# Fused S5 and MLP kernel: the skip D*xn written into PSUM ahead of Y's matmuls, w1's first loads split, a new order by hand

## The chip, the cores and the metric

The kernel runs on one core of a Trainium2 chip. The metric is the device time of one execution in microseconds (us). A core has five engines, each with its own instruction stream: TensorE (PE: matmuls, with weight loads shown as PEld), VectorE (DVE), ScalarE (ACT), GpSimd (POOL) and SyncE (SP, which here only issues transfers). They work side by side and wait for one another through semaphores. Matmuls write to PSUM, which has eight banks of 512 float32 per partition; everything else lies in SBUF. Transfers are done by 16 DMA engines; an instruction on SP or ScalarE only starts one.

## The reference, cut to what matters

```python
def _A_ref(x, Lambda_re, Lambda_im, B_re, B_im, C_re, C_im, log_dt, Dskip):
    Lam = Lambda_re + 1j * Lambda_im
    Lam_bar = jnp.exp(jnp.exp(log_dt) * Lam)
    B_bar = ((Lam_bar - 1.0) / Lam)[:, None] * (B_re + 1j * B_im)
    Bu = jnp.einsum("bld,pd->blp", x + 0j, B_bar)
    for t in range(L):
        h = Lam_bar[None, :] * h + Bu[:, t, :]
        hs.append(h)
    y = 2.0 * jnp.einsum("blp,dp->bld", jnp.stack(hs, 1), C_re + 1j * C_im).real + x * Dskip
    return y

def _B_ref(x, w1, b1, w2, b2):
    h = _gelu(jnp.einsum("bsd,df->bsf", _layernorm(x), w1) + b1)
    return jnp.einsum("bsf,fd->bsd", h, w2) + b2

xn = _layernorm(A_x)
s = _A_ref(xn, ...)
g = _silu(_B_ref(xn, ...))
return A_x + s * g
```

There are L = 2048 tokens, D = 448 channels and F = 1792 hidden units, in bfloat16. D*xn is the last term of y, called the skip here.

## The kernel before, in words

The tokens run in four groups of 512 (g = 0 to 3), each of two blocks of 256. Within a block, even and odd time steps are kept apart ("par"): the recurrence is scanned over pairs of steps, and y is made for even and odd steps by different matrices. All activations are kept transposed, channels on the partitions. 448 channels are three full tiles of 128 (j = 0, 1, 2) and one of 64 (j = 3); the last holds even and odd steps in its two halves of partitions.

What one group goes through:

- norms: `xn` (for the S5 branch) and `xn2` (for the MLP) by VectorE and ScalarE, then a transposing transfer each on SP's queue to `xnT` and `xn2T` (step words L and N).
- the first MLP stage (words m, L661): matmuls of w1 into pairs of PSUM banks, gelu by ScalarE to `gT` (L667). w1 has 448 rows: three tiles of 128, and 64 rows that are loaded by a transfer of their own (key `w1r`); VectorE or ScalarE copies the other 64 rows next to them (keys `w1c_0` to `w1c_3`). Group 0 runs this stage first by blocks, in 256 columns, behind a front of parameter work.
- the second MLP stage (words W, L783 for j < 3, L786 for j = 3): gT times w2, silu by ScalarE to the gate `g_sb` (L789).
- Bu (words b, L690): transposed B (`BT`, three transfers, made from `Bn` and the products `LB`) times xnT. Job 0 reads the first two BT transfers, job 1 the last. ScalarE or VectorE copies the sums to `ue` and `u_sb`.
- the scan (words S): VectorE turns, scans (L749) and turns back; the results are `hx` (odd) and `hz` (even).
- y (words Y, function `yt`): for j < 3 seven matmuls with `CZ` and hx for the odd columns of a bank (L805), seven with `CQ` and hz for the even ones (L806); for j = 3 seven and seven into the two halves of partitions (L813, L814). Then D*xn is added and the sum times the gate is written to `t3`, called t in the profile (L828). In Y0 to Y2, and in one of Y3's four, VectorE adds D*xn while it copies the bank to `tmp` (L826). In the other three of Y3 PE adds it, by a matmul with a diagonal matrix `Dg` of D (L808, L816), which `skips()` builds.
- out: for groups 0 to 2 (words O) two transposing transfers of t back, then VectorE adds x (L842, L845), then output transfers. Group 3 (words P, `out_pe`) is transposed by PE (L855), and VectorE adds x from PSUM (L861); the outputs leave in two pairs, one transfer of each on SP's queue and one on ScalarE's.

Nothing is scheduled while it runs. Every step is a task with keys that it reads and writes; the table `ORDER` gives the order in which the tasks are issued to their engines, and `SECOND` names the tasks that run on the second of their two possible engines. A word of `STEPS` says which task is made: `Y03d2` is y of group 0, tile 3, by VectorE ("d"; "p" is by PE), in bank 2. Each engine works through its own tasks in order, so a task that waits holds back all behind it on its engine, and a transfer on SP's queue those behind it on that queue.

D and b2 come as two rows and are turned into columns `dcol` and `b2c` (together `db`) by small matmuls on PE (`skip_columns`, L554, L555), which stand in the middle of group 0's first MLP stage. The rows are loaded behind all of w1 on SP's queue.

Of the kernel before, what the change touches and what calls it, by code (L numbers as in the profile page):

```python
# [7 lines left out]
ACT = mybir.ActivationFunctionType  # L8
# [189 lines left out]
def bass_recurrent_scan__ssm_conv_s5__mixer_channel_mlp__prompt_kernel(  # L198
# [18 lines left out]
    with ExitStack() as es:  # L217
# [21 lines left out]
        Dg = SB("Dg", [128, 4, 128])  # L239
# [5 lines left out]
        yD = tmp  # L245
# [58 lines left out]
        with nc.Block():  # L304
# [49 lines left out]
            for i, vec in enumerate((A_Dskip, B_b2)):  # L354
                ld("sp", drows[i:i + 1, :], dram_ap(vec, 0, [[D, 1], [1, D]]), [f"dbr{i}"])
# [23 lines left out]
            def first_stats(b):  # L379
                for par in range(2):  # L380
# [5 lines left out]
                    if b == 0:  # L386
                        kb.add("act", [lambda e, var=var, r1=r1: e.activation(r1, var, ACT.Ln, scale=1.0 + LN_EPS, bias=eps[:, 1:2]),
                                       lambda e, r1=r1: e.activation(r1, r1, ACT.Exp, scale=-0.5)], [f"mv0_{q}", "eps", "warm"], [f"r1{q}"], chain=True)
                    elif par == 1:
                        vs2, rs2 = lnmv[:, 0, 1:4:2, 1], lnw[:, 0, 2, 1, 1:4:2]  # L390
                        kb.add("act", [lambda e: e.activation(rs2, vs2, ACT.Ln, scale=1.0 + LN_EPS, bias=eps[:, 1:2]),
                                       lambda e: e.activation(rs2, rs2, ACT.Exp, scale=-0.5)], ["mv0_1", "mv0_3", "eps", "warm"], ["r11", "r13"], chain=True)
# [166 lines left out]
            def skips():  # L559
                for j in range(4):  # L560
                    small(lambda e, j=j: e.tensor_scalar(Dg[:, j, :], ident[:], dcol[:, j:j + 1], None, op0=ALU.mult), ["ident", "db"], [f"Dg{j}"])

            def tables():
# [9 lines left out]
                for k, (dst, src, sc, bias) in enumerate((  # L573
# [6 lines left out]
                        RA + ["rb", "Ws0", "sgn1", "sgn2", "sgn3"], ["W"] + (RA + ["rb"] if k == 4 else []))  # L580
# [3 lines left out]

            tslot = [0]
# [63 lines left out]
            def mm1_phase(g, b, j, pair, second):  # L649
# [9 lines left out]
                def one_mm(k, n, h):  # L659
# [3 lines left out]
                   xk2 + [f"w1_{c}", "w1r"] + ([f"w1c_{c}"] if second else []), [f"ps{bk[0]}", f"ps{bk[1]}"], split=True)  # L663
# [71 lines left out]
            def ssm(g):  # L735
                hb = g % 2
                W, SF = ["W"], ["sf0", "sf1"]
# [53 lines left out]
            ybank = [0]  # L791

            def yt(g, j, by_pe, bk):

                gx = hb = g % 2
                ybank[0] += 1
# [4 lines left out]
                xt_k = [f"xnT{gx}"]  # L801
                ko = [f"hx{hb}", f"hy{hb}"] + [f"CZ{k}" for k in range(7)]
                ke = [f"hz{hb}"] + [f"CQ{k}" for k in range(7)]
                if j < 3:
                    pe([lambda e, k=k: e.matmul(par(psum[:, bk, :], 1), CZ[:, k, cols], halves(hx[:, hb, k, 1:NK + 1]), start=k == 0, stop=k == 6) for k in range(7)], ko, [f"ps{bk}"])  # L805
                    fns = [lambda e, k=k: e.matmul(par(psum[:, bk, :], 0), CQ[:, k, cols], halves(hz[:, hb, k, :]), start=not by_pe and k == 0, stop=not by_pe and k == 6, skip_group_check=by_pe) for k in range(7)]  # L806
                    if by_pe:
                        fns.append(lambda e: e.matmul(P.rearrange("p (q c) -> p q c", q=4), Dg[:, j, :], xr, start=False, stop=True, skip_group_check=True))  # L808
# [162 lines left out]
```

## Time and profile before

| | us |
|---|---|
| median of three runs | 147.08 (147.01 to 148.35) |
| the profiled execution: its span | 145.3 |
| PE busy in it | 138.8 |
| VectorE busy | 130.1 |
| ScalarE busy | 100.5 |
| GpSimd busy | 26.0 |

The profile is of one execution. Its span runs from the first instruction to the last; a run's time also holds what lies around the span. Rows name an instruction by line, engine, operation, and output and input tiles; the name of a tile leaves out its number, so all PSUM banks are "psum", and some buffers carry the name of the memory they share: w_sb is w1 or w2, `xn_sb` both norms, `dk` also holds the rows of D and b2, `Bn` also holds hz and the outputs, and `Cr` also holds the transposed t. "<-" in brackets or behind a bar gives what ended the wait ahead of an instruction. A chain of waits is followed back from the last instruction to what released it.

### The profile page before, as it was taken

The numbers are of one execution on the slowest core, as the hardware profiler recorded it, in microseconds if no ns is written. First come the engines' busy times: TensorE is split into PE (matmuls) and PEld (weight loads), VectorE is DVE, ScalarE is ACT, GpSimd is POOL, SyncE is SP. The second block draws the span as 40 slices with busy tenths as digits, with TensorE's granted clock in tenths as the row PEclk, the third lists the DMA queues.
The fourth block names the chain that finished last, engine by engine and source line by source line (L and its number), as shares of the span: only waits on it lengthen the run. The fifth ranks groups of instructions, "written<-read, shape, count | busy, mean of one in ns | idle before, by whom it ended". The sixth has DMA issues, their size and how long they took to land.

```text
span 145.3 us, 3626 instructions
## 1 busy us (share of the span) xinstructions
PE 138.8 (95%) x1457; PEld 91.9 (63%) x1461; DVE 130.1 (90%) x284; ACT 100.5 (69%) x184; POOL 26.0 (18%) x76
## 2 busy tenths in 40 slices
PE   7879999999999999999999999999999999999990
PEld 7757764464444477776768644877766668744870
DVE  2898999899999799899999999798699999999782
ACT  3588889998889466799999690594559993086200
POOL 4354315154500017000020000300000710000000
PEclk9999999999999999999999999999999999999999
DMA  4959990899999990000000074819800100201434
GB/s 104 299 173 242 351 366 19 162 226 95 210 210 215 122 241 11 5 2 5 0 0 5 18 144 89 163 23 187 192 7 0 68 0 0 82 4 23 95 116 126
DMA packets 38610, 15.98 MB, mean 110 GB/s; under 512 B 33145, under 2 KB 38146, under 8 KB 38594
## 3 DMA queue, kind: packets, MB, share of 16 engines
q1 hardware_dynamic: 38036, 15.52, 48.7%
q10 hardware_dynamic: 558, 0.24, 0.6%
q8 instruction: 11, 0.18, 0.5%
q14 instruction: 5, 0.04, 0.1%
HBM read 5.86 MB, written 1.84 MB: 53 GB/s over the span
## 4 chain that ended last, share of the span: by engine, by line
PE 85%; DVE 4%; DMA 3%; SPq 3%; issue 2%; DVEq 0%
PE psum L661 29%; PE psum L783 25%; PE psum L690 15%; PE psum L805 6%; PE psum L786 4%; PE psum L806 4%; DMA dk<-in_B_b_dram 3%; SPq L78 3%; PE psum L813 2%; DVE t L828 2%; DVE tmp L826 1%; DVE Bn L861 1%; DVE Bn L842 0%; PE psum L855 0%; PE psum L814 0%
## 5 line engine op out<-in xcount | busy, mean ns | idle before, releaser
L661 PE MATMUL psum<-xn2T,w_sb 64*128 64x512 bf16 (+1 forms) x476 | 46.7, 340 | 1.0 <-DVE w_sb L302 0.8
L667 ACT ACTIVATE gT<-psum,b1f 128x512 bf16<-128x512 f32 (+1 forms) x68 | 37.4, 615 | 5.2 <-PE psum L661 5.1
L783 PE MATMUL psum<-gT,w_sb 128*128 128x512 bf16 x164 | 36.2, 379 | 0.4 <-issue 0.3
L661 PEld LDWEIGHTS psum<-xn2T,w_sb 64*128 64x128 bf16 x476 | 25.3, 108 | 15.6 <-PE psum L661 1.4
L783 PEld LDWEIGHTS psum<-gT,w_sb 128*128 128x128 bf16 x168 | 16.2, 98 | 19.8 <-ACT gT L667 1.1
L690 PE MATMUL psum<-xnT,BT 64*128 64x256 bf16 x392 | 24.5, 270 | 0.2 <-DVE tmp L826 0.2
L690 PEld LDWEIGHTS psum<-xnT,BT 64*128 64x128 bf16 x392 | 18.9, 94 | 6.1 <-DVE tmp L826 0.4
L749 DVE TENSOR_TENSOR_SCAN s_w<-vs,dk 128x786 f32<-128x786 bf16 (+1 forms) x8 | 16.3, 2058 | 0.1
L443 ACT ACTIVATE xn_sb<-x_all,lnw 128x448 bf16<-128x448 bf16 (+2 forms) x18 | 11.2, 670 | 5.3 <-DMA xnT<-xn_sb 5.2
L301 ACT ACTIVATE vs<-s_w 64x258 bf16<-64x258 f32 (+2 forms) x12 | 8.0, 686 | 8.0 <-DVE s_w L749 7.9
L789 ACT ACTIVATE g_sb<-psum,db 128x512 bf16<-128x512 f32 (+1 forms) x16 | 9.3, 623 | 4.5 <-PE psum L783 4.4
L826 DVE SCALAR_TENSOR_TENSOR tmp<-xnT,db,psum 128x512 f32<-128x512 bf16 (+1 forms) x16 | 10.1, 645 | 0.9 <-PE psum L814 0.7
L805 PE MATMUL psum<-hx,CZ 128*128 128x256 bf16 x84 | 10.8, 276 | 0.0
L758 POOL TENSOR_TENSOR ang<-s_w,ang 128x16 f32<-128x16 f32 x3 | 1.8, 616 | 49.2 <-ACT s_w L756 49.2
L806 PE MATMUL psum<-Bn,CQ 128*128 128x256 bf16 x84 | 10.5, 273 | 0.0
L465 ACT ACT_TABLE_LOAD x8 | 10.3, 1283 | 0.3
L805 PEld LDWEIGHTS psum<-hx,CZ 128*128 128x128 bf16 x84 | 8.0, 98 | 2.5 <-issue 0.6
L301 ACT ACTIVATE ue<-psum 128x512 bf16<-128x512 f32 (+1 forms) x13 | 6.8, 549 | 3.6 <-PE psum L690 3.6
L806 PEld LDWEIGHTS psum<-Bn,CQ 128*128 128x128 bf16 x84 | 8.1, 98 | 1.4 <-issue 0.4
L301 ACT ACTIVATE u_sb<-psum 128x512 bf16<-128x512 f32 (+1 forms) x14 | 6.0, 490 | 3.5 <-PE psum L690 3.4
L828 DVE TENSOR_TENSOR t<-tmp,g_sb 128x512 bf16<-128x512 f32 (+1 forms) x13 | 7.9, 622 | 0.0
L442 DVE TENSOR_SCALAR xn_sb<-x_all,lnw 128x448 bf16<-128x448 bf16 (+2 forms) x22 | 7.2, 361 | 0.5 <-DMA xnT<-xn_sb 0.3
(155 smaller groups left out, 183.7 us busy)
## 6 DMA issues: line engine op xcount, KB each, us to landing
x_all<-in_A_x_dram SPq DMA_DIRECT2D x3, 448.0 KB, 4.6
w_sb<-in_B_w_dram SPq DMA_DIRECT2D x3, 448.0 KB, 6.4
out_dram<-Bn SPq DMA_DIRECT2D x6, 224.0 KB, 2.4
w_sb<-in_B_w_dram SPq DMA_DIRECT2D x3, 384.0 KB, 5.1
w_sb<-in_B_w_dram SPq DMA_DIRECT2D x2, 224.0 KB, 5.0
Bn<-in_A_B_im_dram SPq DMA_DIRECT2D x1, 336.0 KB, 7.5
Bn<-in_A_B_re_dram SPq DMA_DIRECT2D x1, 336.0 KB, 8.0
x_all<-in_A_x_dram SPq DMA_DIRECT2D x2, 112.0 KB, 2.0
```

Of the source, the lines that this page charges most:

```text
L301: kb.either(("act", [lambda e, o=o, i=i: e.activation(o, i, ACT.Copy) for o, i in pairs]), ("dve", [lambda e, o=o, i=i: e.tensor_copy(o, i ...
L443: ("act", [lambda e, o=o, i=i: e.activation(o, i, ACT.Identity, bias=nb, scale=rs) for o, i in parts]),
L465: kb.add("act", lambda e: e.preload_act_table_set(what), reads, writes, sem=name)
L661: return lambda e: e.matmul(dst(bk[k]), w1_sb[rows, d, fcol(2 * j + k)], rhs[rows, d], start=not second and n == 0, stop=second and n == 3)
L667: act(lambda e, k=k, fi=fi: e.activation(gT[:, gb, fi, cols], psum[:, bk[k], cols], ACT.Gelu_apprx_tanh, bias=b1f[:, fi:fi + 1]), ["b1f", ...
L690: fns.append(lambda e, rows=rows, bank=bank, m=m, o=o, n=n: e.matmul(psum[:, bank, c * NK:(c + 1) * NK].rearrange("p (b c) -> p b c", b=2) ...
L749: dve(lambda e, so=so, vi=vi, di=di: e.tensor_tensor_scan(so, vi, di, 0.0, ALU.add, ALU.mult), ["v", "vl", "vz", "dk", "dk01"] + ["v3"] * ...
L783: pe([lambda e, fi=fi: e.matmul(psum[:, bk, :], w2_sb[:, fi, 128 * j:128 * j + 128], gT[:, gb, fi, :], start=fi == 0, stop=fi == NF - 1) f ...
L805: pe([lambda e, k=k: e.matmul(par(psum[:, bk, :], 1), CZ[:, k, cols], halves(hx[:, hb, k, 1:NK + 1]), start=k == 0, stop=k == 6) for k in ...
L806: fns = [lambda e, k=k: e.matmul(par(psum[:, bk, :], 0), CQ[:, k, cols], halves(hz[:, hb, k, :]), start=not by_pe and k == 0, stop=not by_ ...
L826: dve([lambda e, o=o, p=p, x=x, d=d: e.scalar_tensor_tensor(out=v(o), in0=x, scalar=d, in1=v(p), op0=ALU.mult, op1=ALU.add) for o, p, x, d ...
L828: dve(lambda e: e.tensor_tensor(t3[:, 512 * j:512 * j + n], s, g_sb[:, hb, 512 * j:512 * j + n], ALU.mult), [ks, f"g{hb}_{j}"], [f"t3{j}"])
```

## The change

The new `yt` writes D*xn into the whole bank first, by ScalarE (a copy with the column of D as scale) or by VectorE, whichever `SECOND` says; this is called the seed. All matmuls of y then add to it (none starts a bank anew), and t is read straight from PSUM. The evictions through `tmp`, the matmuls with `Dg`, `Dg` itself and `skips()` are gone. Of the 16 seeds, 14 run on ScalarE and two, the pairs of 64 x 256 of Y1 and Y2, on VectorE; ScalarE's are twelve of 128 x 512 and two pairs of 64 x 256.

The 64 rows of w1 come in two transfers, 768 and 1024 columns wide. SP's queue now starts, behind x, with the 256-column chunk of w1 and the first of these two. D and b2 are issued on ScalarE's queue. The key of the turning tables is split into five, `W0` to `W4`. A branch on `POWER`, which is False, does nothing. `ORDER` and `SECOND` are new throughout.

```diff
-            ld("sp", w1_sb[64:128, 3, :], dram_ap(B_w1, 384 * F, [[F, 64], [1, F]]), ["w1r"])
+            REST = ((0, 768), (768, 1024))
+            def ldrest(k):
+                a, w = REST[k]
+                ld("sp", w1_sb[64:128, 3, a:a + w], dram_ap(B_w1, 384 * F + a, [[F, 64], [1, w]]), [f"w1r{k}"])
             ldw1(0)
+            ldrest(0)
...
-            for c in range(1, 4):
-                ldw1(c)
+            for i, vec in enumerate((A_Dskip, B_b2)):
+                ld("act", drows[i:i + 1, :], dram_ap(vec, 0, [[D, 1], [1, D]]), [f"dbr{i}"])
+            ldw1(1)
+            ldw1(2)
+            ldrest(1)
+            ldw1(3)
...
-            for i, vec in enumerate((A_Dskip, B_b2)):
-                ld("sp", drows[i:i + 1, :], dram_ap(vec, 0, [[D, 1], [1, D]]), [f"dbr{i}"])
...
-            def skips():
-                for j in range(4):
-                    small(lambda e, j=j: e.tensor_scalar(Dg[:, j, :], ident[:], dcol[:, j:j + 1], None, op0=ALU.mult), ["ident", "db"], [f"Dg{j}"])
...
-            def yt(g, j, by_pe, bk):
+            def yt(g, j, bk):
...
+                seeds = [(P, xr, dcol[:, j:j + 1])]
+                if j == 3:
+                    seeds = [(P[h], xnT[h, gx, :, 4 * r + 3, :], dcol[h, 3:4]) for r, h in enumerate((slice(0, 64), slice(64, 128)))]
+                v = lambda t: t.rearrange("p (q c) -> p q c", c=128)
+                kb.either(("act", [lambda e, o=o, x=x, d=d: e.activation(v(o), x, ACT.Copy, scale=d) for o, x, d in seeds]),
+                          ("dve", [lambda e, o=o, x=x, d=d: e.tensor_scalar(v(o), x, d, None, op0=ALU.mult) for o, x, d in seeds]), ["db", f"xnT{gx}"], [f"ps{bk}"])
                 if j < 3:
-                    pe([... start=k == 0, stop=k == 6) for k in range(7)], ko, [f"ps{bk}"])
+                    pe([... start=False, stop=k == 6, skip_group_check=True) for k in range(7)], ko, [f"ps{bk}"])
...
-                    dve([lambda e, o=o, p=p, x=x, d=d: e.scalar_tensor_tensor(out=v(o), in0=x, scalar=d, in1=v(p), op0=ALU.mult, op1=ALU.add) for o, p, x, d in parts],
-                        [f"ps{bk}", "db"] + xt_k, [ks])
-                dve(lambda e: e.tensor_tensor(t3[:, 512 * j:512 * j + n], s, g_sb[:, hb, 512 * j:512 * j + n], ALU.mult), [ks, f"g{hb}_{j}"], [f"t3{j}"])
+                dve(lambda e: e.tensor_tensor(t3[:, 512 * j:512 * j + n], P, g_sb[:, hb, 512 * j:512 * j + n], ALU.mult), [f"ps{bk}", f"g{hb}_{j}"], [f"t3{j}"])
```

Line numbers of the changed kernel are some eight higher behind the loads: L669 is the first MLP stage (L661 before), L698 is Bu (L690), L791 and L794 are the second MLP stage (L783, L786), L812 is a seed by ScalarE, L815 and L816 are y's matmuls (L805, L806), and L675 is gelu.

The new order changes PE's rows most between the first MLP stage of group 1 and that of group 2. Before, PE had there (a row is an instruction, its output and inputs, its shape, and how many follow one another):

```order
L661 MATMUL psum<-xn2T,w_sb 128x512 x98
L783 MATMUL psum<-gT,w_sb 128x512 x42
L786 MATMUL psum<-gT,w_sb 64x256 x28
L690 MATMUL psum<-xnT,BT 128x256 x56
L661 MATMUL psum<-xn2T,w_sb 128x512 x12
L690 MATMUL psum<-xnT,BT 128x256 x42
```

Bu of group 0 came behind all of W1. Now the same place reads:

```order
L669 MATMUL psum<-xn2T,w_sb 128x512 x98
L698 MATMUL psum<-xnT,BT 128x256 x12
L791 MATMUL psum<-gT,w_sb 128x512 x14
L794 MATMUL psum<-gT,w_sb 64x256 x28
L698 MATMUL psum<-xnT,BT 128x256 x44
L791 MATMUL psum<-gT,w_sb 128x512 x28
L698 MATMUL psum<-xnT,BT 128x256 x42
L669 MATMUL psum<-xn2T,w_sb 128x512 x20
```

Twelve of Bu's matmuls moved right behind the first stage, and 44 into the midst of W1.

On SP's queue the transfers that Bu and y need (xnT of group 0; BT; C transposed, as Cr and CZ, from C's rows) stood before in this order:

```order
L77 DMA_TRANSPOSE xn2T<-xn_sb 128x16x128
L78 DMA Bn<-in_A_B_re_dram 64x448
L77 DMA_TRANSPOSE Cr<-in_A_C_re_dram 128x3x448
L78 DMA x_all<-in_A_x_dram 128x2x896
L77 DMA_TRANSPOSE Cr<-in_A_C_im_dram 128x1x448
L77 DMA_TRANSPOSE Cr<-in_A_C_im_dram 128x3x448
L77 DMA_TRANSPOSE CZ<-in_A_C_re_dram 128x1x448
L77 DMA_TRANSPOSE xnT<-xn_sb 128x16x128
L77 DMA_TRANSPOSE BT<-Bn 128x16x128 x2
L77 DMA_TRANSPOSE BT<-Bn 128x24x128
```

Now they stand so:

```order
L77 DMA_TRANSPOSE xn2T<-xn_sb 128x16x128
L78 DMA Bn<-in_A_B_re_dram 64x448
L78 DMA x_all<-in_A_x_dram 128x2x896
L77 DMA_TRANSPOSE xnT<-xn_sb 128x16x128
L77 DMA_TRANSPOSE Cr<-in_A_C_im_dram 128x3x448
L77 DMA_TRANSPOSE Cr<-in_A_C_re_dram 128x3x448
L77 DMA_TRANSPOSE BT<-Bn 128x16x128 x2
L77 DMA_TRANSPOSE Cr<-in_A_C_im_dram 128x1x448
L77 DMA_TRANSPOSE BT<-Bn 128x24x128
L77 DMA_TRANSPOSE CZ<-in_A_C_re_dram 128x1x448
```

xnT moved ahead of all parts of C, one part of C (128x1x448) behind the first two BT transfers, and another, CZ, behind the third.

On ScalarE the stretch from the end of group 2's first MLP stage to the silu table of that group held no work on y before:

```order
L443 ACTIVATE xn_sb<-x_all,lnw 128x128
L667 ACTIVATE gT<-psum,b1f 128x512 x4
L443 ACTIVATE xn_sb<-x_all,lnw 128x384
L443 ACTIVATE xn_sb<-x_all,lnw 128x128
L465 ACT_TABLE_LOAD
```

Now the seeds of Y0, and the first of Y1, stand between the last gelus there (u_sb are copies of Bu's sums):

```order
L675 ACTIVATE gT<-psum,b1f 128x512
L812 ACTIVATE psum<-xnT,db 128x512 x2
L300 ACTIVATE u_sb<-psum 128x2x256
L300 ACTIVATE u_sb<-psum 128x256
L675 ACTIVATE gT<-psum,b1f 128x512
L812 ACTIVATE psum<-xnT,db 128x512
L675 ACTIVATE gT<-psum,b1f 128x512
L812 ACTIVATE psum<-xnT,db 64x256 x2
L675 ACTIVATE gT<-psum,b1f 128x512
L812 ACTIVATE psum<-xnT,db 128x512
L476 ACT_TABLE_LOAD
```

Five seeds moved in among the gelus, ahead of the table load.

More of the change, by code (lines that the diff above doesn't have):

```diff
@@ L244, in bass_recurrent_scan__ssm_conv_s5__mixer_channel_mlp__prompt_kernel @@
         tmp = SB("tmp", [128, 2, 512], F32)
-        yD = tmp
         WT = SB("WT", [128, 4, 3, NW])
@@ L389, in first_stats @@
                     elif par == 1:
[L390 to L392 removed]
+                        vs2, rs2, ws2 = lnmv[:, 0, 1:4:2, 1], lnw[:, 0, 2, 1, 1:4:2], lnw[:, 0, 0, 1, 1:4:2]
+                        if POWER:
+                            kb.add("pool", [lambda e: e.tensor_scalar(ws2, vs2, 1.0 + LN_EPS, LN_EPS * LN_EPS, op0=ALU.mult, op1=ALU.add),
+                                            lambda e: e.tensor_tensor(rs2, ws2, mhalf[:, 0, :].to_broadcast([128, 2]), ALU.pow)], ["mv0_1", "mv0_3", "mhalf"], ["r11", "r13"], chain=True)
+                        else:
+                            kb.add("act", [lambda e: e.activation(rs2, vs2, ACT.Ln, scale=1.0 + LN_EPS, bias=eps[:, 1:2]),
+                                           lambda e: e.activation(rs2, rs2, ACT.Exp, scale=-0.5)], ["mv0_1", "mv0_3", "eps", "warm"], ["r11", "r13"], chain=True)
             def first_apply(b):
@@ L583, in tables @@
                 small([lambda e: e.memset(dk[:, :, 0:1], 0.0), lambda e: e.memset(dk[:, :, 1:LEAD], 1.0), lambda e: e.memset(dk[:, :, LEAD + NK:NS], 0.0)], [], ["dk01"] + old)
+            WK = [f"W{k}" for k in range(5)]
             tslot = [0]
@@ L800, in yt @@
                 xr = xnT[:, gx, :, j::4, :].rearrange("p b r c -> p (b r) c")
-                xt_k = [f"xnT{gx}"]
                 ko = [f"hx{hb}", f"hy{hb}"] + [f"CZ{k}" for k in range(7)]
                 ke = [f"hz{hb}"] + [f"CQ{k}" for k in range(7)]
-                if j < 3:
[L805 to L808, printed above, removed]
-                    pe(fns, ke + (xt_k + [f"Dg{j}"]) * by_pe, [f"ps{bk}"])
+                seeds = [(P, xr, dcol[:, j:j + 1])]
[4 more added lines that the diff above has]
+                          ("dve", [lambda e, o=o, x=x, d=d: e.tensor_scalar(v(o), x, d, None, op0=ALU.mult) for o, x, d in seeds]), ["db", f"xnT{gx}"], [f"ps{bk}"])
+                if j < 3:
+                    pe([lambda e, k=k: e.matmul(par(psum[:, bk, :], 1), CZ[:, k, cols], halves(hx[:, hb, k, 1:NK + 1]), start=False, stop=k == 6, skip_group_check=True) for k in range(7)], ko, [f"ps{bk}"])
+                    pe([lambda e, k=k: e.matmul(par(psum[:, bk, :], 0), CQ[:, k, cols], halves(hz[:, hb, k, :]), start=False, stop=k == 6, skip_group_check=True) for k in range(7)], ke, [f"ps{bk}"])
                 else:
@@ L812, in yt @@
                     for k in range(7):
[L813 to L828 removed]
+                        fns += [lambda e, k=k: e.matmul(psum[0:64, bk, 0:NK], CQ[:, k, cols], hz[:, hb, k, :], start=False, stop=k == 6, skip_group_check=True),
+                                lambda e, k=k: e.matmul(psum[64:128, bk, 0:NK], CZ[:, k, cols], hx[:, hb, k, 1:NK + 1], start=False, stop=k == 6, skip_group_check=True)]
+                    pe(fns, ko + ke, [f"ps{bk}"], split=True)
+                dve(lambda e: e.tensor_tensor(t3[:, 512 * j:512 * j + n], P, g_sb[:, hb, 512 * j:512 * j + n], ALU.mult), [f"ps{bk}", f"g{hb}_{j}"], [f"t3{j}"])
             OLD = [f"CQ{k}" for k in range(7)] + [f"CZ{k}" for k in range(7)]
@@ L880, in bass_recurrent_scan__ssm_conv_s5__mixer_channel_mlp__prompt_kernel @@
             first_stats(1)
-            gelu_table(0, ["cr", "r10", "r12", "r11", "r13"])
+            gelu_table(0, ["cr", "r10", "r12"] + ["r11", "r13"] * (not POWER))
             dummies(4, ["st0"])
```

36 lines of the change are left out of this document (10 added, 26 removed), and 36 rows, old and new, of the table ORDER.

## The prediction

> **What bounds the kernel now.** I read the page's busy line and its chain of what ended last, then the list of PE's waits, then a table by stage. Columns of the page's first line: busy us, share of the span, instructions.
>
> ```profile
> PE 138.8 (95%) x1457; PEld 91.9 (63%) x1461; DVE 130.1 (90%) x284; ACT 100.5 (69%) x184; POOL 26.0 (18%) x76
> PE 85%; DVE 4%; DMA 3%; SPq 3%; issue 2%; DVEq 0%
> ```
>
> PE is busy 95% of the span and is 85% of the chain. What it waited for (us in total, times, longest):
>
> ```profile
> PE psum L661 <- DVE w_sb L302: 0.8, 1, 0.8
> PE psum L554 <- DMA dk<-in_B_b_dram: 0.8, 1, 0.8
> PE psum L855 <- DVE t L828: 0.3, 1, 0.3
> PE psum L690 <- DVE tmp L826: 0.2, 1, 0.2
> ```
>
> The two waits of 0.8 us are both in the front, before 10.5 us; behind it PE has almost no holes. By stage (stretch, its length, then busy time of PE, PEld, DVE, ACT, POOL with instructions, clock, DMA share, GB/s):
>
> ```profile
> 5.40:10.50 5.10, 3.47 (x57) 2.64 (x55) 4.91 (x21) 4.03 (x10) 2.46 (x11) 1.00 0.78 209
> 20.70:31.40 10.70, 10.70 (x71) 5.46 (x72) 9.63 (x33) 10.50 (x16) 4.21 (x17) 1.00 0.63 134
> 31.40:42.50 11.10, 10.88 (x99) 5.22 (x97) 10.59 (x29) 9.38 (x16) 4.05 (x8) 1.00 1.12 184
> 42.50:53.30 10.80, 10.80 (x71) 5.35 (x72) 9.83 (x23) 7.77 (x12) 0.00 (x0) 1.00 1.19 193
> 53.30:74.70 21.40, 21.40 (x295) 15.03 (x296) 20.05 (x36) 18.52 (x34) 4.38 (x9) 1.00 0.08 16
> 91.00:97.60 6.60, 6.44 (x71) 5.02 (x68) 5.60 (x12) 5.06 (x9) 1.36 (x2) 1.00 0.50 97
> ```
>
> So work taken off VectorE is worth only what PE waits for it: 0.16 us in 91.00:97.60 (6.60 − 6.44). To move the end, an edit must start PE sooner, shorten PE's own work, or open a hole in it. The granted clock is 1.00 throughout. The profiled span is 145.3 us and the median of the three runs 147.08, so 1.8 us lie around the span; I keep those.
>
> **The front.** The timeline of all engines there, two rows of the chain (SP issues the 384 KB chunk at 2.19 and w1's last 64 rows at 2.67), and the sizes and landing times of three loads of w1:
>
> ```profile
> 2.19 0.43 SPq L78
> ...
> 2.67 0.59 SPq L78
> w_sb<-in_B_w_dram SPq DMA_DIRECT2D x1, 384.0 KB, 4.2
> w_sb<-in_B_w_dram SPq DMA_DIRECT2D x1, 224.0 KB, 4.8
> w_sb<-in_B_w_dram SPq DMA_DIRECT2D x1, 192.0 KB, 4.6
> 5.64 0.60 ACT L301 ACTIVATE xn2T<-psum 128x512 bf16<-128x512 bf16 x1 [0.41 <-PE psum L406]
> 6.80 0.42 DVE L302 COPY xn2T<-psum 128x512 bf16<-128x512 bf16 x1
> 7.25 0.29 DVE L302 COPY w_sb<-w_sb 64x512 bf16<-64x512 bf16 x1
> 7.50 1.90 PEld L661 LDWEIGHTS psum<-xn2T,w_sb 64*128 64x128 bf16 x34 [0.88 <-issue]
> 9.02 1.57 ACT L667 ACTIVATE gT<-psum,b1f 128x256 bf16<-128x256 f32 x4
> 10.48 0.21 PE L554 MATMUL psum<-ident,dk 2*128 2x2 bf16 x3 [0.81 <-DMA dk<-in_B_b_dram]
> ```
>
> PE's first weight load (7.50) comes before the DVE copy named as releaser ends (7.25 + 0.29 = 7.54), so that copy isn't it: the 64 rows are, 2.67 + 4.8 = 7.47. They were third behind the 384 KB chunk. Now 192 KB and 96 KB lead, 320 KB less. From the chunk's landing (issued at 2.19, so 6.4) to 7.47 224 KB took 1.07 us, 4.8 ns per KB; 320 KB less would give about 6.0. Next late is the second copy of xn2T, at 7.22 (6.80 + 0.42) on VectorE. It now runs on ScalarE straight behind the first, and ScalarE does the two rsqrt pairs before the parameter copy; I take 0.3 to 0.6 us off the transposes ahead, so the copies end near 6.6. PE starts near 6.7, 0.85 us sooner (bounds: 0.3, if only 7.22 is reached, and 1.5). The wait of 0.81 for b2 goes too, since D and b2 are issued on ScalarE's queue some 2 us sooner. But PE can't keep it: gelu began at 9.02, behind its table load, frees the three pairs of banks only from there on, and the copies of w1's 64 rows stand on VectorE behind the norm of the second tile. I expect the same 84 first matmuls to end 0.85 us sooner in all; bounds 0 (if those set the pace) and 1.7 (0.85 + 0.81). **Front: −0.85.**
>
> The Trainium skill's page "DMA: Bandwidth & Descriptors", section "Issuing engines are not separate DMA queues", speaks against the move of D and b2: loads from several engines share the same 16 DMA engines and only the issue time is saved. By it they might land near 10.3 as before (10.48 in the row above) and PE would stall again by some 0.2 us, which makes the sum 147.1; whether the small rows really overtake no run here shows.
>
> **Y and its seed.** Groups by form: busy us and mean ns behind the bar.
>
> ```profile
> L826 DVE SCALAR_TENSOR_TENSOR tmp<-xnT,db,psum 128x512 f32<-128x512 bf16 x10 | 7.2, 744 | 0.2
> L826 DVE SCALAR_TENSOR_TENSOR tmp<-xnT,db,psum 64x256 f32<-64x256 bf16 x6 | 2.9, 479 | 0.7 <-PE psum L814 0.7
> L594 ACT ACTIVATE tmp<-Bn,cw 128x512 f32<-128x512 bf16 x1 | 0.7, 709 | 0.0
> L301 ACT ACTIVATE ue<-psum 128x512 bf16<-128x512 f32 x10 | 6.0, 598 | 3.6 <-PE psum L690 3.6
> L301 ACT ACTIVATE u_sb<-psum 128x256 bf16<-128x256 f32 x7 | 2.4, 380 | 2.5 <-PE psum L690 2.4
> ```
>
> Removed from VectorE: 7.2 + 2.9 = 10.1 us of evictions; the four small builds of Dg, on VectorE and POOL and waited for by nobody in PE's list, go as well. Added: 16 seeds. Twelve of 128x512 and two pairs of 64x256 go to ScalarE, two pairs to VectorE (4 x 0.48 = 1.9 us). No such write into PSUM is in the trace. The nearest rows are L594 (same scale by a column, written to SBUF, 709) and L301 (598, without the scale); I take 0.65. ScalarE gets 12 x 0.65 + 4 x 0.38 = 9.3 us. VectorE's relief is worth the waits that name it: **−0.2**, bounds 0 and −0.5 (with L855's 0.3).
>
> A seed puts a link into the bank's cycle: before, Y's first matmul waited for the bank's last reader; now the seed waits for it, and the matmul for the seed. In Y2 and Y3 ScalarE has room. In 53.30:74.70 it is busy 18.52 of 21.40, so 2.9 us are free, and Y0's four seeds need 3 x 0.65 + 2 x 0.38 = 2.7. They fit with 0.2 to spare, behind gelu in queue order, where PE also has less Bu work left to cover. A stall here lies between 0 and those 2.7 us (a gain isn't possible, as PE has no hole there); as the work just fits, **+0.2**.
>
> **The tail.** The first and the last piece of the chain that bear on it:
>
> ```profile
> 138.72 0.23 PE psum L808
> ...
> 142.28 0.29 DVE Bn L861
> ```
>
> One Dg matmul of 0.23 lies on the chain, and a second 512-wide one follows before the last sum ends at 142.57. At most 2 x 0.23 goes, and the first t no longer has an eviction in front. But all Y matmuls now stand ahead of all the transposes, the first pair of output DMAs waits for them, and each queue takes the second only after the first. **−0.1**, bounds −0.5 and +0.2.
>
> **The B transposes.** The new order puts twelve Bu matmuls right behind group 1's first MLP stage and 44 in the midst of W1; before, Bu of group 0 came after all of W1. Chain rows for where PE stood, then SP's queue, then BT's summary (first and last issue) and landing times:
>
> ```profile
> 42.49 9.15 PE psum L783 x41
> 51.63 1.65 PE psum L786 x28
> 53.28 3.17 PE psum L690 x56
> 24.51 2.75 SPq L77 DMA_TRANSPOSE xn2T<-xn_sb  x1
> 30.04 3.29 SPq L77 DMA_TRANSPOSE Cr<-in_A_C_im_dram  x2
> 33.37 1.26 SPq L77 DMA_TRANSPOSE CZ<-in_A_C_re_dram  x1
> 34.67 3.98 SPq L77 DMA_TRANSPOSE xnT<-xn_sb  x1
> 38.70 8.70 SPq L77 DMA_TRANSPOSE BT<-Bn  x3
> L77 SPq DMA_TRANSPOSE BT<-Bn x3: 1868/2627/4122, 38.7 to 43.3; - x3
> DMA to landing us min/median/max: 4.5/5.1/8.0
> ```
>
> Bu needed all three BT parts at 53.28; the last was issued at 43.3 and landed 8.0 later, at 51.3, 2 us ahead. Now the first twelve need two parts at about 42.49 − 0.85 − 0.3 = 41.3 (the front, and PE's holes in 31.40:42.50). Job 1 needs the last after those twelve (12 x 3.17/56 = 0.7), 14 matmuls of L783 (14 x 9.15/41 = 3.1) and the 1.65 of L786: 46.7. The queue has also been turned: xnT comes first, CZ (1.26) goes behind all parts, and Ct3, of the same shape, behind the first two. SP issues back to back, so these come out sooner by 2 x 1.26 = 2.5 us, and all of it by the 1.1 that I take xmT1 to be sooner (the front's 0.85, and ten small sine steps gone from VectorE to POOL). The second part, issued at 38.7 + 1.87 = 40.6 and landed 5.1 later: 45.7 − 3.6 = 42.1, a stall of 0.8. The last: 51.3 − 1.1 − 1.26 = 48.9, if it still takes 8.0 us; with the median 5.1, 46.0; need, after that stall, 47.5, which is half-way. Stall in all: 0 (all in time) to 3.3 (if xmT1 is no sooner, 50.0). I take **+0.8**: the early two as computed, and the last nearer to the median row, since one transfer less is queued ahead of it.
>
> "DMA: Bandwidth & Descriptors", section "Latency and other measured facts" of the Trainium skill, gives 261 GB/s for such transposes. The stage table shows 184 to 193 where they run; by the page they would all be in time and the sum would be 146.1.
>
> **Sum.** −0.85 − 0.2 + 0.2 − 0.1 + 0.8 = −0.15 on 145.3, with the 1.8 around it 146.9 us.
>
> **Rivals.**
> *The last B transpose is late.* One transfer, one place: PE in front of Bu's job 1 in W1. For it: DMA share 1.12 and 1.19 from 31.40 to 53.30. Against: one transfer less ahead of it. It decides once it lands after 49.2, 2.5 us past need; if it lands at 50.0 the time is 146.9 − 0.8 + 3.3 = 149.4. Chance 0.18, nearly all of it over the bound.
> *ScalarE becomes the bound around Y0.* All of Y0's seeds uncovered: 146.9 − 0.2 + 1.4 (half of 2.7) = 148.1. Its 20.70:31.40 row, 10.50 of 10.70, speaks for it, the room elsewhere against. Chance 0.12.
> *Everything fits.* B lands in time, seeds are covered, the front keeps 1.2 and the tail 0.4: 147.08 − 1.2 − 0.2 − 0.4 = 145.3. For it: PE's order has no hole by itself. Chance 0.2.
> *Front bound elsewhere.* PE's start moves, but gelu's banks and the copies take all of it: 147.7. Chance 0.1.
>
> **Numbers.** My own case has 0.4 and gives 146.9. The bound is 1%, 1.47 us, about what a measurement can tell from no change. Faster comes from "everything fits", 0.2; slower from the late transpose, 0.18; the other three, 0.62, are within. The range goes from the time of "everything fits", half of which may lie below it, to 148.8, which takes in the cases of ScalarE and of the front and a late transpose of up to 2.7 us; about 2 in 10 is left out.
>
> **What would show it.** Right: PE's first 64-row matmuls near 6.7 and no wait on dk; no L826 group; ScalarE some 9 us busier, VectorE some 8 less busy; a PE wait on BT under 1 us near 41. Wrong: PE still starting at 7.2 or later; a PE wait on BT of over 2 us; waits on seeds (a scaled copy into psum) ahead of the odd-row matmuls of Y0; a hole before the last outputs.

## The result, and the profile after

| | before | changed |
|---|---|---|
| median, us (20 runs each) | 147.95 | 149.38 |
| lowest to highest, us | 147.01 to 148.47 | 147.85 to 150.84 |
| span of the profiled execution, us | 145.3 | 147.9 |

The ratio of the changed kernel to the one before, run side by side, is 1.0086, with a 95% interval of 1.0063 to 1.011. The change made the kernel 0.9% slower, some 1.3 us; the forecast was 146.9 us, 0.1% faster. Ratios here use fast runs alone, which leaves out the changed kernel's longest, 150.84 us at a granted clock of 0.989. The profiled execution before took 147.08 us, close to the shortest of its runs, and that of the changed kernel 149.62, close to the middle of its own; so the two profiled spans lie 2.6 us apart, twice what the ratio gives.

The page's busy line and chain of the changed kernel:

```profile
PE 138.6 (94%) x1452; PEld 91.8 (62%) x1457; DVE 123.2 (83%) x266; ACT 107.1 (72%) x195; POOL 23.9 (16%) x83
PE 69%; ACT 13%; DMA 9%; DVE 3%; issue 2%; SPq 2%; DVEq 0%
```

PE does the same work (138.6 against 138.8 us), VectorE 6.9 us less, ScalarE 6.6 more. But the chain has 69% of PE in it instead of 85%, and 13% of ScalarE, which it didn't have. PE's waits in the changed kernel:

```profile
PE psum L669 <- DMA w_sb<-in_B_w_dram: 1.4, 1, 1.4
PE psum L815 <- DVE hx L775: 1.4, 1, 1.4
...
PE psum L791 <- ACT gT L675: 0.5, 2, 0.4
PE psum L816 <- DVE Bn L776: 0.4, 1, 0.4
```

The first is in the front (w1's 512-column chunk). The second and the last stand ahead of Y1: PE waits 1.4 us for hx and 0.4 us for hz (which lies in Bn), where the kernel before waited 0.16 us in the whole stage. No wait on BT is listed, none on a seed, and none for D or b2.

To see where the 2.6 us between the two profiled spans arise, take the same marks in both chains: the start of W0, of Y1, of Y3, and the end. Before:

```profile
20.68 9.01 PE psum L783 x41
91.02 1.57 PE psum L805 x14
134.84 1.57 PE psum L805 x14
```

After:

```profile
21.17 9.01 PE psum L791 x41
137.10 1.57 PE psum L815 x14
```

Y1's first matmuls aren't on that chain; PE's timeline has them, behind W2's:

```profile
82.55 9.01 PE L791 MATMUL psum<-gT,w_sb 128*128 128x512 bf16 x41
92.94 1.74 PE L815 MATMUL psum<-hx,CZ 128*128 128x256 bf16 x14 [1.37 <-DVE hx L775]
```

W0 starts 0.49 us later. Y1 could have started at 91.56 (82.55 + 9.01) and starts at 92.94. From Y3 to the end it is 147.9 − 137.1 = 10.8 us instead of 145.3 − 134.84 = 10.46. So, in these two executions, 0.49 is in the front, 1.4 + 0.4 ahead of and in Y1, and 0.34 in the tail: 2.6 us.

Why Y1 waits is read on ScalarE and VectorE. S1's scan (L757) leaves its results in `s_w`; ScalarE copies them to `vs` (L300), and VectorE makes hx from that. ScalarE between group 2's table load and the gates, changed kernel:

```profile
81.90 1.28 ACT L476 ACT_TABLE_LOAD   x1
85.39 0.76 ACT L454 ACTIVATE xn_sb<-x_all,lnw 128x448 bf16<-128x448 bf16 x1 [2.20 <-DMA xnT<-xn_sb]
86.17 0.20 ACT L763 ACTIVATE s_w<-s_w 64x1 f32<-64x1 f32 x1
86.39 0.20 ACT L764 ACTIVATE s_w<-s_w 64x1 f32<-64x1 f32 x1
86.61 0.76 ACT L454 ACTIVATE xn_sb<-x_all,lnw 128x448 bf16<-128x448 bf16 x1
87.28 1.49 ACT L300 ACTIVATE vs<-s_w 128x1548 bf16<-128x1548 f32 x1
88.67 0.67 ACT L812 ACTIVATE psum<-xnT,db 128x512 f32<-128x512 bf16 x1
89.28 0.67 ACT L797 ACTIVATE g_sb<-psum,db 128x512 bf16<-128x512 f32 x1
89.85 0.68 ACT L812 ACTIVATE psum<-xnT,db 128x512 f32<-128x512 bf16 x1
90.47 0.46 ACT L797 ACTIVATE g_sb<-psum,db 128x256 bf16<-128x256 f32 x1
90.82 1.26 ACT L300 ACTIVATE vs<-s_w 128x258 bf16<-128x258 f32 x3
```

VectorE around it:

```profile
81.08 4.02 DVE L757 TENSOR_TENSOR_SCAN s_w<-vs,dk 128x1048 f32<-128x1048 bf16 x2
...
86.79 0.39 DVE L453 TENSOR_SCALAR xn_sb<-x_all,lnw 128x448 bf16<-128x448 bf16 x1
...
88.80 0.97 DVE L771 TENSOR_TENSOR pa<-vs,WT 128x1548 bf16<-128x1548 bf16 x1 [0.95 <-ACT vs L300]
...
92.58 0.29 DVE L775 TENSOR_TENSOR hx<-pa 128x258 bf16<-128x258 bf16 x1
92.91 0.99 DVE L813 TENSOR_SCALAR psum<-xnT,db 64x256 f32<-64x256 bf16 x2
93.93 1.09 DVE L776 TENSOR_TENSOR Bn<-hx,ue 128x1792 bf16<-128x1792 bf16 x1
```

The scan ends at 81.08 + 4.02 = 85.10, but the copy starts at 87.28. In ScalarE's queue two pieces of group 3's xn (L454) stand ahead of it. The first waits for xnT's transfer, since it overwrites what that transfer reads, to 85.39; with the second and the two small copies that carry the scan's state on (L763, L764), the main copy is 2.2 us late. A third piece of xn, on VectorE (L453), stands ahead of hx too, but VectorE then idles 0.95 us until the main copy ends, so that piece holds up nothing. Then two seeds and two gates (88.67 to 90.82) stand ahead of the last three copies, and on VectorE a pair of seeds (0.99) ahead of hz. In the kernel before, the copies came straight behind the scan, and the xn piece that waits for xnT came last. Its wait of 5.22 us held up the gates behind it on ScalarE, but cost PE nothing:

```profile
83.67 2.67 ACT L301 ACTIVATE vs<-s_w 128x1548 bf16<-128x1548 f32 x4 [1.34 <-DVE s_w L749]
...
92.43 0.76 ACT L443 ACTIVATE xn_sb<-x_all,lnw 128x448 bf16<-128x448 bf16 x1 [5.22 <-DMA xnT<-xn_sb]
```

So the theory (A) is that the new order of ScalarE's queue, with the xn pieces ahead of the scan's copies, costs PE the wait at Y1. The rivals: the seeds between the copies do it (B), or the scan itself ends later (C). The experiments are set against these, and against two theories for the front: D, the small loads of D and b2 on ScalarE's queue hold up w1, and E, w1's 512-column chunk is late because it is issued third.

### The profile page after: what moved, and what is told of

The parts are those of the page before. It is cut to its first block, busy times and chain, and to the rows that moved or that the text cites. A ratio compares the mean times of both kernels' runs of the same rounds, so it can differ in the third digit from the quotient of the medians.

```text
span 147.9 us, 3604 instructions
## 1 busy us (share of the span) xinstructions
PE 138.6 (94%) x1452; PEld 91.8 (62%) x1457; DVE 123.2 (83%) x266; ACT 107.1 (72%) x195; POOL 23.9 (16%) x83
## 4 chain that ended last, share of the span: by engine, by line
PE 69%; ACT 13%; DMA 9%; DVE 3%; issue 2%; SPq 2%; DVEq 0%
PE psum L669 24%; PE psum L791 18%; PE psum L698 12%; ACT gT L675 5%; PE psum L816 5%; DMA w_sb<-in_B_w_dram 4%; DMA xnT<-xn_sb 4%; PE psum L815 4%; PE psum L794 3%; ACT psum L812 3%; ACT vs L300 2%; PE psum L820 2%; SPq L78 2%; ACT xn_sb L454 1%; ACT u_sb L300 1%
## 5 line engine op out<-in xcount | busy, mean ns | idle before, releaser
L669 PE MATMUL psum<-xn2T,w_sb 64*128 64x512 bf16 (+1 forms) x476 | 46.5, 339 | 1.8 <-DMA w_sb<-in_B_w_dram 1.4
L675 ACT ACTIVATE gT<-psum,b1f 128x512 bf16<-128x512 f32 (+1 forms) x68 | 37.4, 614 | 6.9 <-PE psum L669 6.7
L791 PE MATMUL psum<-gT,w_sb 128*128 128x512 bf16 x163 | 36.2, 379 | 0.8 <-ACT gT L675 0.5
L669 PEld LDWEIGHTS psum<-xn2T,w_sb 64*128 64x128 bf16 x476 | 25.4, 108 | 16.5 <-DMA w_sb<-in_B_w_dram 1.7
L791 PEld LDWEIGHTS psum<-gT,w_sb 128*128 128x128 bf16 x168 | 16.2, 98 | 19.3 <-ACT gT L675 0.4
L698 PE MATMUL psum<-xnT,BT 64*128 64x256 bf16 x392 | 24.6, 269 | 0.0
L698 PEld LDWEIGHTS psum<-xnT,BT 64*128 64x128 bf16 x392 | 18.8, 94 | 6.4 <-issue 0.6
L757 DVE TENSOR_TENSOR_SCAN s_w<-vs,dk 128x1048 f32<-128x1048 bf16 (+1 forms) x8 | 16.3, 2058 | 0.1
L823 DVE TENSOR_TENSOR t<-psum,g_sb 128x512 bf16<-128x512 f32 (+1 forms) x16 | 9.7, 619 | 4.2 <-PE psum L816 3.9
L815 PE MATMUL psum<-hx,CZ 128*128 128x256 bf16 x84 | 10.9, 275 | 1.4 <-DVE hx L775 1.4
L300 ACT ACTIVATE vs<-s_w 64x258 bf16<-64x258 f32 (+2 forms) x14 | 8.0, 571 | 5.6 <-DVE s_w L757 5.5
L300 ACT ACTIVATE ue<-psum 128x512 bf16<-128x512 f32 (+1 forms) x12 | 6.1, 546 | 7.9 <-PE psum L698 7.8
L816 PE MATMUL psum<-Bn,CQ 128*128 128x256 bf16 x84 | 10.8, 273 | 0.4 <-DVE Bn L776 0.4
L812 ACT ACTIVATE psum<-xnT,db 128x512 f32<-128x512 bf16 (+1 forms) x16 | 9.9, 636 | 1.7 <-DVE t L823 1.6
L453 DVE TENSOR_SCALAR xn_sb<-x_all,lnw 128x448 bf16<-128x448 bf16 (+2 forms) x27 | 8.6, 365 | 2.5 <-DMA xnT<-xn_sb 2.4
L454 ACT ACTIVATE xn_sb<-x_all,lnw 128x448 bf16<-128x448 bf16 (+2 forms) x13 | 8.5, 688 | 3.0 <-DMA xnT<-xn_sb 3.0
L815 PEld LDWEIGHTS psum<-hx,CZ 128*128 128x128 bf16 x84 | 7.9, 98 | 3.9 <-DVE hx L775 1.9
L797 ACT ACTIVATE g_sb<-psum,db 128x512 bf16<-128x512 f32 (+1 forms) x16 | 9.8, 627 | 0.7 <-PE psum L791 0.5
L766 POOL TENSOR_TENSOR ang<-s_w,ang 128x16 f32<-128x16 f32 x2 | 0.7, 360 | 56.8 <-ACT s_w L764 56.8
L816 PEld LDWEIGHTS psum<-Bn,CQ 128*128 128x128 bf16 x84 | 8.0, 98 | 2.1 <-DVE Bn L776 0.7
L371 DVE BATCH_NORM_STATS2 lnst<-x_all 128x6 f32<-128x448 bf16 x12 | 7.1, 615 | 0.1
```

Source lines behind the costliest of these rows:

```text
L300: kb.either(("act", [lambda e, o=o, i=i: e.activation(o, i, ACT.Copy) for o, i in pairs]), ("dve", [lambda e, o=o, i=i: e.tensor_copy(o, i ...
L454: ("act", [lambda e, o=o, i=i: e.activation(o, i, ACT.Identity, bias=nb, scale=rs) for o, i in parts]),
L669: return lambda e: e.matmul(dst(bk[k]), w1_sb[rows, d, fcol(2 * j + k)], rhs[rows, d], start=not second and n == 0, stop=second and n == 3)
L675: act(lambda e, k=k, fi=fi: e.activation(gT[:, gb, fi, cols], psum[:, bk[k], cols], ACT.Gelu_apprx_tanh, bias=b1f[:, fi:fi + 1]), ["b1f", ...
L698: fns.append(lambda e, rows=rows, bank=bank, m=m, o=o, n=n: e.matmul(psum[:, bank, c * NK:(c + 1) * NK].rearrange("p (b c) -> p b c", b=2) ...
L757: dve(lambda e, so=so, vi=vi, di=di: e.tensor_tensor_scan(so, vi, di, 0.0, ALU.add, ALU.mult), ["v", "vl", "vz", "dk", "dk01"] + ["v3"] * ...
```

## The experiments

All kernels are the changed one with the edit shown, unless said otherwise; in `ORDER` a task is a number, and the edits move a few. Each was run 12 times, the kernel without seeds six times. A ratio is always to the kernel before.

### The xn pieces behind the scan's copies

```diff
 ScalarE's order from the table load on
-xn piece, carry copies, xn piece, vs (main), seed, gate, seed, gate, vs (3 small)
+carry copies, vs (main), seed, gate, seed, gate, vs (3 small), xn piece, xn piece
 VectorE's order
-xn piece ahead of hx, ..., seeds, hz
+seeds, hz, xn piece
```

> The changed kernel, with group 3's first two pieces of xn on ScalarE moved behind the copies of S1's scan (the one on VectorE goes behind hz). Theory A (ScalarE's order: the two xn pieces hold up the scan's copies while they wait for xnT's transfer): PE's waits for hx and hz ahead of Y1, 1.4 + 0.4 us in the changed kernel, go to about 0, and the time falls by some 1.7 us, a ratio near 0.997 to the kernel before. Rival B (the seeds between those copies hold them up): the waits stay above 1 us and the ratio stays near 1.008. Rival C (the hold-up is VectorE's scan, which ends later in itself): as B.

Ratio 0.993, interval 0.9897 to 0.9963, 1.6% below the changed kernel's 1.0086. That is 2.3 us, more than the 1.7 expected, whose 0.997 lies just outside the interval; in the profiles the time from W0's start to the end falls by some 2 us, from 126.7 to 124.9 (145.7 − 20.8). PE's waits now name neither hx nor hz; these two, both in the front, lead the list:

```profile
PE psum L669 <- DMA w_sb<-in_B_w_dram: 1.2, 2, 0.6
PE psum L669 <- ACT gT L675: 0.9, 1, 0.9
```

ScalarE's timeline shows the main copy at the scan's end, with the seeds still where they were:

```profile
85.03 1.50 ACT L300 ACTIVATE vs<-s_w 128x1548 bf16<-128x1548 f32 x1 [1.27 <-DVE s_w L757]
86.44 0.67 ACT L812 ACTIVATE psum<-xnT,db 128x512 f32<-128x512 bf16 x1
...
88.59 1.26 ACT L300 ACTIVATE vs<-s_w 128x258 bf16<-128x258 f32 x3
89.88 1.41 ACT L454 ACTIVATE xn_sb<-x_all,lnw 128x448 bf16<-128x448 bf16 x2
```

Theory A holds, and B and C fall as causes of their own: with all the seeds in place and a scan that ends at the same time (85.0), the wait is gone. This kernel, all of the change with three pieces of xn moved, is 0.7% faster than the kernel before.

### The seeds behind the scan's copies, the xn pieces left

```diff
 ScalarE's order from the table load on
-xn piece, carry copies, xn piece, vs (main), seed, gate, seed, gate, vs (3 small)
+xn piece, carry copies, xn piece, vs (main), vs (3 small), seed, gate, seed, gate
```

> The changed kernel, with the last three copies of S1's scan moved ahead of the two seeds and two gates on ScalarE that stood between; the xn pieces stay. Theory A: the first copy still starts late, so hx still ends near 92.4 instead of 92.9 us and PE's wait for hx falls only from 1.4 to some 0.8 us; ratio near 1.005. Rival B (seeds): both waits go, 1.7 us less, ratio near 0.997. Rival C: no change, 1.008.

Ratio 1.0084, interval 1.0045 to 1.0123: no better than the changed kernel in time. The profile shows the part of the gain that theory A leaves to the seeds:

```profile
PE psum L815 <- DVE hx L775: 0.9, 1, 0.9
...
PE psum L816 <- DVE Bn L776: 0.4, 1, 0.4
```

The wait for hx fell from 1.4 to 0.9, as expected (0.8), so the seeds add half a microsecond as long as the xn pieces stand ahead. That doesn't show in the times, whose interval is 0.6 us either way: expected was 1.005, and 1.0084 is the ratio that rival C gave. C fell only by the kernel above.

### The rows of D and b2 on SP's queue again

```diff
-                ld("act", drows[i:i + 1, :], dram_ap(vec, 0, [[D, 1], [1, D]]), [f"dbr{i}"])
+                ld("sp", drows[i:i + 1, :], dram_ap(vec, 0, [[D, 1], [1, D]]), [f"dbr{i}"])
```

In `ORDER` the two go behind w1's last chunk.

> The changed kernel, with the rows of D and b2 loaded on SP's queue behind all of w1 again. Theory D (the two small loads on ScalarE's queue hold up w1's second chunk): the chunk lands near 7.7 instead of 9.9 us, PE's wait of 1.4 us for it goes, and PE waits up to 0.8 us for b2 instead; W0 starts 0.5 to 1 us sooner than in the changed kernel. Rival E (the chunk is late because it is issued third, behind 288 KB of w1): it lands near 9.9 us as before, the wait stays at 1.4 us, and the ratio stays near 1.009 or rises by the wait for b2.

Ratio 1.0102, interval 1.0062 to 1.0142. Two lines of PE's waits:

```profile
PE psum L669 <- DMA w_sb<-in_B_w_dram: 0.8, 1, 0.8
PE psum L565 <- DMA dk<-in_B_b_dram: 0.8, 1, 0.8
```

The chunk landed at 9.5 us (3.3 + 6.2), so it can be late without the small loads on ScalarE's queue: theory D falls as the cause. Whether they add something no run separates from the spread shown below. The wait of 0.8 us for b2 is back, so this part of the change does what it says in the profile. The Trainium skill's "DMA: Bandwidth & Descriptors", section "Issuing engines are not separate DMA queues", says that another issuing engine saves only issue time. The two don't conflict: the gain here is from when the rows are issued, at 2.5 and 2.8 us, ahead of most of w1.

### w1's loads in the old order

```diff
 SP's queue behind x
-256-column chunk, 64 rows (768), 512-column chunk
+512-column chunk, 64 rows (768), 256-column chunk
```

PE's first five steps of the first MLP stage, and VectorE's copies of 64 rows, go in the order that matches.

> The changed kernel, with w1's 512-column chunk issued first again, then its first 64 rows, then the 256-column chunk, and PE's first matmuls in the old order to match. Theory E (order of issue): the 512-column chunk lands near 6.4 us as in the kernel before, PE starts near 7.3 us and doesn't wait for w1 over 0.5 us; W0 starts about 1 us sooner than the 21.2 us of the changed kernel, ratio near 1.002. Theory D: w1's loads are still held up, the last to land does so near 9.9 us, and the wait only moves; ratio near 1.009.

Ratio 1.0053, interval 1.0023 to 1.0083. The 512-column chunk lands 4.0 us after issue, and PE runs its first 48 matmuls without a break:

```profile
w_sb<-in_B_w_dram SPq DMA_DIRECT2D x1, 384.0 KB, 4.0
7.14 3.33 PE L669 MATMUL psum<-xn2T,w_sb 64*128 64x256 bf16 x48 [0.32 <-ACT cw L495]
```

W0 started at 19.6 us here. That is what theory E expects of the profile, but the time fell by half of what it expects (1.0053, not 1.002). Its interval and the changed kernel's overlap, and the next part shows why one profile of a front doesn't settle it. Part of the gain was lost again further on: from W0's start to the end it was 127.4 us (147.0 − 19.6) instead of 126.7. With PE sooner, the BT wait of the prediction appeared:

```profile
41.75 0.83 PE L698 MATMUL psum<-xnT,BT 64*128 64x256 bf16 x12 [0.50 <-DMA BT<-Bn]
```

### How much the front varies

Three kernels above have the same front instruction for instruction: the changed one and the two that edit S1. Issue to landing of the 512-column chunk, issued at 3.3 us in each, in that order:

```profile
w_sb<-in_B_w_dram SPq DMA_DIRECT2D x1, 384.0 KB, 6.6
```

```profile
w_sb<-in_B_w_dram SPq DMA_DIRECT2D x1, 384.0 KB, 5.5
```

```profile
w_sb<-in_B_w_dram SPq DMA_DIRECT2D x1, 384.0 KB, 4.2
```

It landed at 9.9, 8.8 and 7.5 us, and W0 started at 21.2, 20.9 and 19.3. So the 1.4 us that PE waited for it in the changed kernel's profile is one draw. (Where a row of W0 says x41, the first of its 42 matmuls isn't in the trace, and the start is read some 0.2 us late: 21.2 here, but not the other two.) The kernel before was profiled a second time:

> The kernel before once more, for its profile. If the front's loads vary from execution to execution in it as they do in the changed kernel (W0 at 21.2, 20.8 and 19.3 us with the same front), the 64 rows of w1 or the start of W0 stand elsewhere by 0.5 us or more (7.5 and 20.7 us in the first profile); if only the new order of loads varies, they stand within 0.2 us.

Its chain has W0 here, and its PE waits for xn2T at the start and only 0.3 us for b2:

```profile
20.19 9.01 PE psum L783 x41
```

W0 came 0.49 us sooner than in its first profile, and the span was 144.8 instead of 145.3, just as much shorter. Behind W0's start it was 124.6 us both times, so what varied there was the front. That is just at the 0.5 us that the expectation set for a front that varies; the 64 rows landed at 7.0 us (2.67 + 4.3) instead of 7.5.

### Both repairs, and the tail

The next kernel joins the moved xn pieces and the old order of w1's loads.

> The changed kernel with two repairs together: group 3's first xn pieces behind the copies of S1's scan on ScalarE, and w1's chunks loaded, and first used by PE, in the old order. If the two places are independent, the gains add: 0.993 from the first, and 0.3% from the second (1.0053 against 1.0086), so a ratio near 0.990 to the kernel before, no PE wait for hx, and W0 starting near 19.6 us. If the earlier front only makes PE meet the B transposes sooner, a wait for BT of 0.5 us or more shows near 42 us and the ratio stays at 0.993.

Ratio 0.9927, interval 0.9895 to 0.996: the same as with the xn pieces alone, and not the 0.990 of gains that add up. Nor did the wait for BT come that the other case named. In its profile PE starts in good time (6.87 us), and then waits for the next thing in the front, the transposed second half of xn2T:

```profile
PE psum L669 <- DMA xn2T<-xn_sb: 1.4, 1, 1.4
```

W0 starts at 21.0 us, not at the expected 19.6. The order of w1's loads is thus worth nothing that these runs resolve. A further kernel adds another order of the tail to both:

```diff
 PE, from Y3's second tile on
-y (all), transposes of t2, t0, t3, t1
+y1, transposes of t0, y2, transposes of t1, y3, transposes of t2 and t3
 VectorE
-t0, t1, t2, t3, sum 2, sum 0, sum 1, sum 3
+t0, t1, sum 0, sum 1, t2, sum 2, t3, sum 3
```

> As the kernel with both repairs, and in the tail PE's transposes of each t, and VectorE's sums, stand right behind that t again, so that the first pair of output transfers leaves before the last matmuls of y. Theory T (the tail lost its gain since both pairs of outputs are issued together): the first pair is issued near 6 us behind W3's end instead of 7.2, and the time from W3's end to the end of the span falls from 10.8 to about 10.3 us, a ratio 0.003 below the other kernel's. Rival: the last pair's own 2 to 3 us set the end, and nothing changes.

Ratio 0.9914, interval 0.9884 to 0.9944. The changed kernel issued both pairs of outputs (x2 on each queue) together; here the first pair goes at 140.11. ScalarE's issues, first of the changed kernel, then of this one:

```profile
144.24 1.39 ACTq L78 DMA_DIRECT2D out_dram<-Bn  x2
```

```profile
140.11 2.36 ACTq L78 DMA_DIRECT2D out_dram<-Bn  x2
```

Y3 starts at 134.49 and the span ends at 144.6: 10.1 us, against 10.8 in the changed kernel and 10.46 before. The profile bears theory T out; the difference of the two ratios, 0.0013, is inside their intervals, and the medians lie the other way (146.46 and 146.60 us), so the gain isn't shown in the time. This is the lowest ratio of all, 0.9% below the kernel before.

### Without seeds

```diff
-                kb.either(("act", [... e.activation(v(o), x, ACT.Copy, scale=d) ...]), ("dve", [...]), ["db", f"xnT{gx}"], [f"ps{bk}"])
+                dve([... e.scalar_tensor_tensor(out=v(o), in0=x, scalar=d, in1=v(o), op0=ALU.mult, op1=ALU.add) ...], ["db", f"xnT{gx}"], [f"ps{bk}"])
```

This is an edit of the kernel with both repairs. The added line stands behind the matmuls, which start their banks themselves. Since it reads xnT later than a seed does, the transposes that overwrite xnT come later in `ORDER` too: that of group 2 is issued at 87.8 us instead of 78.7.

> As the kernel with both repairs, but without seeds: the matmuls of y start their banks themselves, and VectorE adds D*xn in place in PSUM behind them, right ahead of each t; xnT of groups 2 and 3 is transposed after that. VectorE gets some 10 us more and ScalarE 9.9 less. Theory V (VectorE's relief is worth little, since PE sets the time): PE waits for hx or hz by no more than 0.5 us in all, ratio within 0.003 of the kernel with both repairs. Rival (the new order lives on that relief): S1's scan starts some 2.5 us later, PE waits 2 us or more ahead of Y1, ratio above 1.005.

Ratio 1.0497, interval 1.0439 to 1.0555, 5.7% above the kernel with both repairs. PE's waits:

```profile
PE psum L815 <- DVE hx L775: 3.0, 2, 1.7
PE psum L851 <- DVE t L824: 2.2, 2, 1.5
PE psum L698 <- DVE t L824: 0.9, 1, 0.9
PE psum L698 <- DVE u_sb L721: 0.8, 1, 0.8
```

The rival holds: the new order lives on VectorE's relief. The run doesn't say that the seeds alone are worth 5.7%, for this order wasn't made for evictions, the transposes moved with them, and the kernel before hid nearly all of its evictions; it says that order and seed can't be priced one without the other.

## Why the prediction was wrong, point by point

**The step that failed** is a term put at nothing without a reason: what the new order of ScalarE's queue between S1's scan and Y1 costs PE. The prediction looked for holes that the new order could open at two places, ahead of Bu (B transposes) and ahead of Y0 (seeds). It never priced Y1, where two pieces of xn now stand ahead of the scan's copies, and two seeds among them. It called ScalarE free enough by its busy time in the stage of Y0; the loss came from the order of its queue one stage on. The missing term measured 1.4 + 0.4 us of PE's waits in the profile, and moving the pieces behind the copies took 1.6% off the time. The −0.2 for VectorE's relief isn't what failed: PE's wait for tmp, which it named, is gone.

As an estimate, take the forecast's −0.85 and −0.2, nothing for seeds and B transposes, +0.34 for the tail and +1.8 for Y1: that is +1.1 us, near the measured 1.3. By luck the forecast wasn't further off: its +0.2 and +0.8, for two waits that didn't come, stood in for part of the one that did.

**The front, −0.85.** In the changed kernel's profile PE started at 7.34 us instead of the forecast 6.7, and the second copy of xn2T, named there as next in line, ended at 7.20 and not near 6.6. That is one draw too: in the two other profiles of the same front the copy ended at 6.57 and 6.52, and PE started at 7.06 and 6.66. The 64 rows landed at 6.58 (2.68 + 3.9), later than the forecast 6.0. What the step left out is the 512-column chunk, now issued third, for which PE waited 1.4 us, 0.6 us and not at all in the three. In the first profile the loss at W0 was 0.49.

What the front does on average can only be inferred. Behind W0's start the changed kernel's profile took 126.7 us and the one before 124.6, 2.1 us more. If that were the same in every execution (it was in the kernel before, twice), the measured 1.3 us would leave −0.8 for the front, and the interval −0.5 to −1.2. It isn't quite the same: with w1's old order, where nothing behind the front is changed, it was 127.4 us, 0.5 of it the wait for BT. So the term may have been right in size, but this is argued from sums, not shown; the direct profiles go from −1.2 to +0.5.

**D and b2.** Right: no wait for either, and the wait of 0.8 us came back when they were put back.

**Seeds at Y0, +0.2.** PE's list has no wait for a seed. Each cost more than taken:

```profile
L812 ACT ACTIVATE psum<-xnT,db 128x512 f32<-128x512 bf16 x12 | 8.0, 691 | 1.7 <-DVE t L823 1.6
L812 ACT ACTIVATE psum<-xnT,db 64x256 f32<-64x256 bf16 x4 | 1.9, 469 | 0.1
```

691 ns, near the 709 of the scaled copy to SBUF rather than the 598 of the plain copy out of PSUM, and 469 for a half, where 380 was taken. The total was 9.9 us instead of 9.3. PE waited for none of it at Y0. ScalarE as a whole became 6.6 us busier, not some 9. The rival "ScalarE becomes the bound around Y0" was right about the engine and wrong about the place and, but for the half microsecond of the seeds at Y1, about the work.

**The B transposes, +0.8.** Its mechanism is real and its size too large. The first BT transfer went out at 33.8 instead of 38.7, sooner than the 35.1 (38.7 − 3.6) that the sum took, and there was no wait in the changed kernel, 0.5 us in the kernel with w1's old order and in the one with the tail. The rival "the last B transpose is late" didn't come: in no profile did PE wait for the last part. The stretch 31.80:42.60 of the changed kernel moved 174 GB/s, no more than the 184 to 193 of before, so it was the sooner issue that got them there, and not a higher rate. The Trainium skill's 261 GB/s for transposes with a non-contiguous middle dimension ("DMA: Bandwidth & Descriptors", "Latency and other measured facts") would also have had them all in time, but this trace doesn't reach it.

**The tail, −0.1.** It became +0.34. VectorE's last sum came 7.3 us behind Y3's start (144.41 − 137.10), 0.4 sooner than before (142.57 − 134.84 = 7.7), as the prediction's upper gain had it. But the outputs are issued from 144.2 on, both pairs one behind the other, and the span ends 3.7 us after; before, the first pair had gone at 141.4, and only one was left when the last sum ended. The prediction had named this ("each queue takes the second only after the first") and priced it too low.

## What to carry to other kernels

When a table of order is rewritten, walk each engine's queue for an instruction that waits for a transfer or another engine, and ask what now stands behind it. In the profile of before it is the row with idle ahead of it and a releaser: such a row can cost nothing at the end of a queue, as here, and costs its wait, and its own time, to everything it is moved in front of. An engine's spare time in a stage says nothing on this; pieces of 0.76 us that nobody was waiting for held up the copy that the scan, and then PE, depended on.

## What the runs showed of the hardware that wasn't expected

One and the same sequence of loads at the start, in three kernels that differ only 80 us later, took from 4.2 to 6.6 us for its 384 KB chunk and moved the start of W0 by some 1.7 us. The kernel before varies in the same place, though less in the two profiles there are (0.49 us). Why stays open: the chunk took 6.2 us also without the loads of D and b2 on ScalarE's queue, with w1's old order the chunk landed in 4.0 us in one profile, and no run tried the split of the 64 rows, or the narrow chunk, by itself.

Matmuls that add to a bank which ScalarE has written ahead take no longer than those that start it themselves: y's odd-row and even-row matmuls of j < 3 took 275 and 273 ns each on average, 276 and 273 before.
